# Attention and gated-MLP block on one core: the first loads regrouped, the query weights' means added on VectorE, a longer warm-up on a constant

## The chip, the core and the metric

The kernel runs on one core of a Trainium2 chip. TensorE (PE) multiplies matrices into PSUM; VectorE (DVE), ScalarE (ACT) and GpSimd (POOL) work on SBUF, the first two on PSUM too; SyncE (SP) issues nearly all transfers. The engines run side by side and wait for one another on semaphores. The metric is the device time of one execution in microseconds (us). Three runs of the kernel before took 281.43, 282.21 and 282.88 us, median 282.21.

## The reference

One sequence of 2048 rows of 640, 32 heads of 20. LN is a layer norm without gain or bias; all tensors are bf16.

```
qkv   = LN(x) @ wqkv                         # 640 x 1920
phi(u)= [softmax(u @ w_phi), softmax(-u @ w_phi)]   # 20 + 20 features per head, for q and for k
kv    = sum over rows of phi(k)^T v ,  z = sum over rows of phi(k)
o     = phi(q) kv / (phi(q) z + 1e-6)
h     = x + o @ wo
out   = h + ((LN(h) @ w_gate) * (LN(h) @ w_up)) @ w_down     # 640 x 1536, 1536 x 640
```

## The kernel before, in words

The rows are cut into 16 tiles of 128 (t = 0 to 15) and four blocks of four tiles; the width of 640 into five chunks of 128.

*Weights first.* Since the feature map is linear before its softmax, the kernel multiplies w_phi into the key and query weights once. For the keys (`wk_rounds`, L637) five chunks of the key weights are loaded into `Wnat`, transposed on TensorE against an identity, centred (the mean of each column over the input width is subtracted, which does the layer norm's subtraction of the mean), and multiplied by a block-diagonal `Phi` in the rounds x0 to x4; `evac` (L751) copies each result to `Wp`. For the queries the transposed weights come from five transposing loads (t0 to t4, `wqT`, L1018) into `WT[:, 0]`; `wq_means` (L721, unit wm) makes the column means on TensorE, and ScalarE spreads them over a 128 x 640 tile `nmu`. Each of the rounds y0 to y4 (`wq_round`, L728) then runs twelve matmuls: six on `WT`, six that add the means through `nmu`. The value weights are loaded straight into `Wp`, summed on TensorE (`wv_sums`, unit wv) and centred in place on VectorE (c0 to c4, L776).

*Rows.* x arrives transposed, one transposing load per tile (`load_xT`, L503; lT4 and so on), and again untransposed by blocks (lx0 to lx3). `stats` (units s0, s2, s4, s8, s12) makes the sums and squares of tiles: TensorE, a few small VectorE operations, then seven small GpSimd operations that give each row's scale `rs`. `keys` (k0 to k15) projects a tile (ten matmuls of 320 columns), takes the row's largest absolute value on VectorE (L806, L809), and ScalarE makes two exponentials (L813). The K units sum each head's 40 features on VectorE (L824), invert (L826), and GpSimd multiplies the 128 x 1280 tile (L827). `values` (v0 to v15) projects and ScalarE scales. The units A0 to A14 add up the key-value sums on TensorE, Aout copies them to `KVsb` on VectorE (L893, L896). Queries (q, Q), the quotient (n), the output projection and residual (h), gate and up (f) and down (d, e) follow per block; transposes between them go over SyncE's transposing loads, for tiles 0 and 1 over TensorE.

*What sets the order.* Each engine's order is written out by hand in `ORDER` (L58): a list of unit names per engine, where a name that stands several times stands for that unit's successive operations. `Prog.place` (L200) walks these lists with an assumed duration `t` and latency `lat` for each operation, and settles with them which buffer of a pool an operation gets; the order on an engine is the list's alone. There are four PSUM buffers of two banks. At most eight plain loads and eight transposing loads are in flight, each on a semaphore of its own. Engines issue in order, so an operation that waits holds everything behind it on its engine.

The first units of SyncE's list are all in the unit `in`: five loads of one key-weight chunk each, the value weights in two loads, then the transposed x of tiles 0 to 3. ScalarE issues one load, w_phi. TensorE begins with `warm` (L572): 26 matmuls of 128 columns on the tile `ones`, which GpSimd fills first.

Of the kernel before, what the change touches and what calls it, by code (L numbers as in the profile page):

```python
# [5 lines left out]
FP32 = mybir.dt.float32  # L6
# [5 lines left out]
P = 128  # L12
# [60 lines left out]
    "DVE":  # L73
# [12 lines left out]
    "ACT":  # L86
# [9 lines left out]
    "POOL":  # L96
# [37 lines left out]
class Op:  # L134
    __slots__ = ("eng", "idx", "emit", "deps", "dma", "waits", "vc", "signal", "tick", "sem", "val",
                 "n", "dur", "lat", "bufs", "succ", "start", "end", "open", "bytes", "unit")


class Prog:
# [13 lines left out]
    def op(self, eng, emit, rd=(), wr=(), app=(), dma=None, t=0.2, lat=None, use=(), after=(), size=0.0):  # L153
        o = Op()
        o.eng, o.emit, o.dma = eng, emit, dma
# [44 lines left out]
    def place(self):  # L200
# [20 lines left out]
        while len(order) < len(ops):  # L221
# [29 lines left out]
            if o.dma is not None:  # L251
                land = max(s + 2.3, fabric) + o.bytes
                fabric = land
                o.end = land + o.lat
                flight.setdefault(o.dma[0], []).append(o.end)
            else:
                o.end = s + o.lat
# [119 lines left out]
def _build(ctx, nc, A_x, A_wqkv, A_w_phi, A_wo, B_w_gate, B_w_up, B_w_down, out):  # L377
# [43 lines left out]
    nmean = sb([P, NC], FP32, "nmean")  # L421
    Ssum = sb([P, 2, 2 * H], FP32, "Ssum")
# [9 lines left out]
    nmu, nmuk = [outb[:, k, :].rearrange("p (a n) -> p a n", a=NC) for k in range(2)]  # L432
# [31 lines left out]
    def load(out_, in_, wr, mb, after=(), eng="SP", app=()):  # L464
        return g.op(eng, lambda e: e.dma_start(out_, in_), wr=wr, app=app, after=after, dma=("w", 8), t=0.5, lat=0.4, size=mb / 0.38)  # L465

    def transpose(out_, in_, rd, wr, use=(), t=1.27, size=1.07):

        return g.op("SP", lambda e: e.dma_start_transpose(out_(), in_()), rd=rd, wr=wr, use=use, dma=("tr", 8), t=t, lat=0.5,  # L469
                    size=size)  # L470
# [27 lines left out]
    def load_wnat(w, cs=(0, NC), eng="SP"):  # L498
        c0, c1 = cs
        load(Wnat[:, c0:c1, :], A_wqkv[P * c0:P * c1, D * w:D * (w + 1)].rearrange("(c p) n -> p c n", p=P), R_Wnat[c0:c1],  # L500
             0.16 * (c1 - c0), eng=eng)

    def load_xT(t):  # L503
        transpose(lambda: xT[:, t, :, 0:P], lambda: A_x[0, P * t:P * (t + 1), :], [], [R_xT[t]], t=1.27, size=0.8 if t < 2 else 1.4)

    def load_x(b):
        load(x_all[:, 4 * b:4 * b + 4, :], A_x[0, 4 * P * b:4 * P * (b + 1), :].rearrange("(t p) n -> p t n", p=P), [R_x[b]], 0.64)

    def load_wv(c0, c1):
        load(Wp[:, c0:c1, 2 * D:3 * D], A_wqkv[P * c0:P * c1, 2 * D:3 * D].rearrange("(c p) n -> p c n", p=P), R_Wp[2][c0:c1], 0.16 * (c1 - c0))  # L510

    U("in")
    load(Wrows[:, :, :], A_w_phi.rearrange("h d f -> (h d) f").rearrange("(a p) f -> p a f", p=P), [R_Wrows], 0.03, eng="ACT")
    for c in range(NC):
        load_wnat(1, (c, c + 1))
    load_wv(0, 2)
# [587 lines left out]
```

## Time and profile before

| what | value |
|---|---|
| median of three runs | 282.21 us |
| the profiled execution | 281.24 us, span 279.4 us |
| mean granted TensorE clock | 1.000 |
| TensorE busy | 274.6 us (98%), 2257 matmuls |
| VectorE busy | 165.5 us (59%) |
| ScalarE busy | 133.4 us (48%) |
| GpSimd busy | 106.3 us (38%) |
| transfers | 28.08 MB, mean 100 GB/s |

The span runs from the first to the last instruction of the profiled execution; the 1.8 us between it and the execution's time lie around it. "Busy" is the union of an engine's instructions. Matmuls overlap one another in a pipeline, so a matmul's mean length (299 ns at 320 columns) is longer than the distance from one to the next. In rows of the chain, "SPq" is SyncE's queue of issues and "DMA" the time that a transfer is awaited. Idle time that is shown with "<-" was ended by the instruction behind the arrow.

### The profile page before, as it was taken

What the parts mean: (1) busy time and instruction counts of PE and PEld (TensorE: products, weight loads), DVE (VectorE), ACT (ScalarE), POOL (GpSimd) and SP (SyncE); (2) the same over time, 40 slices, a digit from 0 to 9 for tenths busy, and PEclk for the clock granted to TensorE, in tenths of its full rate; (3) what the DMA queues carried; (4) which work ended last, traced back from release to release, by engine and by line L of the source; (5) the groups of instructions that cost most, each with busy time, mean ns of one, the idle gap of its engine ahead of it and who ended that gap; (6) DMA issues with size and microseconds to landing.
All of it is one profiled execution on the core that took longest, in us unless ns stands there. A gap on an engine that the chain in (4) does not pass through costs nothing.

```text
span 279.4 us, 5540 instructions
## 1 busy us (share of the span) xinstructions
PE 274.6 (98%) x2257; PEld 187.7 (67%) x2257; DVE 165.5 (59%) x313; ACT 133.4 (48%) x227; POOL 106.3 (38%) x156
## 2 busy tenths in 40 slices
PE   8999999999999999999999999999999999999996
PEld 7777778778878888877746655676454444456773
DVE  2999999999899798688528474431141132315011
ACT  2477999998566346363271432401444342410321
POOL 5348899999620322233300680002521034000321
PEclk9999999999999999999999999999999999999999
DMA  7989989404964378946530065561210001000112
GB/s 192 166 170 140 214 125 397 137 2 94 302 78 94 74 180 150 280 99 91 122 73 2 7 136 72 116 98 45 72 49 0 0 0 49 0 0 2 70 48 72
DMA packets 65241, 28.08 MB, mean 100 GB/s; under 512 B 55744, under 2 KB 63936, under 8 KB 65216
## 3 DMA queue, kind: packets, MB, share of 16 engines
q1 hardware_dynamic: 64560, 27.70, 45.8%
q8 instruction: 18, 0.29, 0.5%
q10 hardware_dynamic: 656, 0.03, 0.2%
q14 instruction: 7, 0.06, 0.1%
HBM read 11.82 MB, written 2.62 MB: 52 GB/s over the span
## 4 chain that ended last, share of the span: by engine, by line
PE 94%; SPq 3%; DMA 2%; DVE 1%; issue 0%
PE ps L568 93%; SPq L469 2%; DMA xT<-in_A_x_dram 2%; SPq L465 1%; PE ps L480 0%; DVE outb L1010 0%; DVE KVsb L893 0%; DVE rden L927 0%; DVE KVsb L896 0%
## 5 line engine op out<-in xcount | busy, mean ns | idle before, releaser
L568 PE MATMUL ps<-phik,Wgu 128*128 128x512 bf16 (+1 forms) x600 | 107.6, 336 | 0.0
L568 PEld LDWEIGHTS ps<-phik,Wgu 128*128 128x128 bf16 x600 | 58.2, 98 | 43.6 <-DVE phik L969 1.2
L969 DVE TENSOR_TENSOR phik<-ps,gate 128x512 bf16<-128x512 f32 (+1 forms) x60 | 34.0, 575 | 61.2 <-PE ps L568 60.3
L568 PE MATMUL ps<-Wp,xT 128*128 128x320 bf16 x480 | 68.4, 299 | 0.0
L967 ACT ACTIVATE gate<-ps 128x512 bf16<-128x512 f32 (+1 forms) x60 | 30.1, 512 | 70.4 <-PE ps L568 56.5
L568 PE MATMUL ps<-vaug,phik 128*128 128x320 bf16 (+3 forms) x544 | 60.2, 270 | 0.0
L568 PEld LDWEIGHTS ps<-Wp,xT 128*128 128x128 bf16 x480 | 46.2, 98 | 17.1
L568 PEld LDWEIGHTS ps<-vaug,phik 128*128 128x128 bf16 x544 | 43.4, 97 | 15.9
L985 POOL TENSOR_TENSOR outb<-t,x_all 128x640 bf16<-128x640 f32 x12 | 16.8, 1397 | 88.0 <-ACT t L982 85.7
L827 POOL TENSOR_TENSOR phik<-phik,Rk 128x1280 bf16<-128x1280 bf16 x16 | 37.3, 2357 | 0.7 <-DVE nb L809 0.6
L982 ACT ACTIVATE t<-ps,mh,rs 128x640 f32<-128x640 f32 x12 | 10.6, 882 | 41.4 <-PE ps L568 41.4
L806 DVE TENSOR_REDUCE ps<-ps 128x1 f32<-128x640 f32 x32 | 26.2, 819 | 3.5 <-PE ps L568 3.1
L846 DVE TENSOR_REDUCE Sq<-eq 128x64 f32<-128x1280 bf16 x16 | 23.5, 1474 | 1.6 <-ACT eq L813 1.6
L824 DVE TENSOR_REDUCE Ssum<-phik 128x64 f32<-128x1280 bf16 x16 | 23.4, 1471 | 0.1
L857 POOL TENSOR_TENSOR eq<-eq,rq 128x640 bf16<-128x640 bf16 x16 | 20.3, 1270 | 0.9
L852 POOL TENSOR_TENSOR rq<-Sq,rq 128x32 f32<-128x32 f32 x16 | 4.0, 255 | 39.8 <-DVE rq L851 39.8
L813 ACT ACTIVATE eq<-ps,nb,rs 128x640 bf16<-128x640 f32 x16 | 14.1, 883 | 10.1 <-DVE nb L809 9.3
L813 ACT ACTIVATE phik<-ps,nb,rs 128x640 bf16<-128x640 f32 x16 | 14.0, 884 | 3.1 <-DVE nb L809 3.0
L561 ACT ACTIVATE junk<-x_all 128x640 bf16<-128x640 bf16 x20 | 14.7, 735 | 0.0
L833 ACT ACTIVATE vaug<-ps,rs 128x640 bf16<-128x640 f32 x16 | 12.8, 801 | 3.5 <-PE ps L568 3.5
L813 ACT ACTIVATE eq<-ps,nb,nrs 128x640 bf16<-128x640 f32 x16 | 14.1, 882 | 0.0
L946 DVE SCALAR_TENSOR_TENSOR x_all<-ps,mh,x_all 128x640 bf16<-128x640 f32 x16 | 13.9, 874 | 0.4
(83 smaller groups left out, 226.4 us busy)
## 6 DMA issues: line engine op xcount, KB each, us to landing
x_all<-in_A_x_dram SPq DMA_DIRECT2D x4, 640.0 KB, 9.0
out_dram<-outb SPq DMA_DIRECT2D x15, 160.0 KB, 1.8
Wgu<-in_B_w_up_dram SPq DMA_DIRECT2D x1, 1920.0 KB, 11.3
Wgu<-in_B_w_gate_dram SPq DMA_DIRECT2D x1, 1920.0 KB, 8.2
vaug<-in_B_w_down_dram SPq DMA_DIRECT2D x1, 1920.0 KB, 8.5
phiqT<-in_A_wqkv_dram SPq DMA_DIRECT2D x5, 160.0 KB, 3.8
phiqT<-in_A_wqkv_dram SPq DMA_DIRECT2D x1, 800.0 KB, 6.0
Wo<-in_A_wo_dram SPq DMA_DIRECT2D x1, 800.0 KB, 5.6
```

The lines of the kernel that those rows point to most:

```text
L561: g.op("ACT", lambda e: e.activation(out=junk[:, v.i, :], in_=in_, func=func, accum_out=acc), rd=rd, wr=wr, use=[v], t=0.73, lat=0.97)
L568: ins = e.matmul(o_, lhsT=l_, rhs=r_, start=s_, stop=p_, skip_group_check=True)
L806: g.op("DVE", lambda e: e.tensor_reduce(out=mx(), in_=PS[v.i][:, :, 0:HALF], axis=AX.XY, op=ALU.max, apply_absolute_value=True, negate=Tru ...
L813: g.op("ACT", lambda e, s=s, sc=sc: e.activation(out=signed(dst(), s), in_=PS[v.i][:, :, 0:HALF].rearrange("p b (h f) -> p b h f", f=DH), ...
L824: g.op("DVE", lambda e: e.tensor_reduce(out=Ssum[:, vs.i, :], in_=x, axis=AX.X, op=ALU.add), rd=R_phik[t], wr=vs.R, use=[vs], t=1.39, lat=1.5)
L827: g.op("POOL", lambda e: e.tensor_tensor(out=x, in0=x, in1=Rk[:, vr.i, :].unsqueeze(2).to_broadcast([P, 2 * H, DH]), op=ALU.mult), rd=vr.R ...
L846: g.op("DVE", lambda e: e.tensor_reduce(out=Sq[:, vs.i, :], in_=eq[:, b.i, :].rearrange("p (g f) -> p g f", f=DH), axis=AX.X, op=ALU.add), ...
L857: return e.tensor_tensor(out=x, in0=x, in1=rq[:, vr.i, :].unsqueeze(2).to_broadcast([P, H, DH]), op=ALU.mult)
L946: g.op("DVE", lambda e: e.scalar_tensor_tensor(out=xv, in0=PS[v.i][:, :, 0:HALF], scalar=mh[:, t:t + 1], in1=xv, op0=ALU.subtract, op1=ALU ...
L967: g.op("ACT", lambda e: e.activation(out=gate[:, vg.i, 0:P * n], in_=PS[v.i][:, 0, 0:P * n], func=ACT.Copy), rd=[v.R[0]], wr=vg.R, use=[v, ...
L969: g.op("DVE", lambda e: e.tensor_tensor(out=hhT[:, hb, ft, sl], in0=PS[v.i][:, 1, 0:P * n], in1=gate[:, vg.i, 0:P * n], op=ALU.mult), rd=[ ...
L985: g.op("POOL", lambda e: e.tensor_tensor(out=outb[:, vo.i, :], in0=t32[:, v3.i, :], in1=x_all[:, t, :], op=ALU.add), rd=v3.R + [R_h[t]], w ...
```

## The change

1. The first loads are regrouped. The key weights' five chunks come as three loads: chunks 0 and 1, and chunk 4, on SyncE; chunks 2 and 3 on ScalarE's queue, ahead of w_phi. x of tiles 0 and 1 follows on SyncE, then the value weights in one load, then x of tiles 2 and 3.
2. The query weights' means stay a column of five numbers, `nmeanq`, which ScalarE copies from PSUM. VectorE adds them to the transposed query weights in place, one add of 128 x 640 for each of five chunks (units wq0 to wq4). The tile `nmu` is gone, and a round y runs six matmuls instead of twelve.
3. The warm-up is 34 matmuls, on a constant tile that is there from the start.
4. `Prog.place` assumes other latencies for loads (and given landing times for the first ones), and the five written-out orders are new throughout. On SyncE the query weights (lwq, t0 to t4) now come before x of tiles 8 to 15.

The core of the diff; the orders are cut to their first lines:

```diff
 ORDER = {
     "PE":
-        "warm wk wk wk wk wk wk wk wk wk wk x1 wv x1 x0 x3 wv x0 s0 s0 x2 x4 k0 k0 k0 s2 k0 k0 s2 k1 k3 v1 k2 s4 s4 s4 s4 "
-        "k6 k4 v5 k7 v6 k5 v3 s8 s8 s8 s8 k8 v4 wm v11 k9 v10 k10 s12 v7 s12 s12 s12 y4 y0 y1 y3 k11 y2 k14 v2 q1 q0 v12 "
...
+        "warm wk wk wk wk wk wk wk wk wk wk x1 s0 s0 x1 x0 x3 x0 wv wv x2 s2 x4 s2 k0 k0 k0 k0 k0 k1 k2 v1 s4 s4 s4 s4 k3 "
+        "k5 v6 wm k6 v7 k7 v2 v5 k4 y4 y3 y2 y0 y1 v4 q1 q0 s12 s12 s12 s8 s8 s12 s8 s8 v0 k13 v10 k8 v8 k9 v13 v9 k11 "
...
     "DVE":
-        "wk in in in in in wk wk wk wk x1 x3 c0 s0 s0 s0 c3 c1 c2 s2 s2 s2 k0 k0 c4 k1 k1 k3 K0 k3 k2 k2 s4 s4 s4 s4 s4 "
-        "K1 K0 k4 K1 k4 k6 K3 k6 k7 K3 k7 K2 k5 K2 k5 s8 s8 s8 s8 s8 K4 k8 K4 K6 k8 K5 k9 K6 k9 K8 k10 K5 k10 s12 K7 K8 "
...
+        "wk in in in in in wk wk wk wk s0 s0 s0 x3 x1 c4 c1 s2 c3 s2 s2 k0 c2 k0 c0 k1 k2 k1 K0 s4 k2 s4 s4 K0 s4 k3 s4 "
+        "k3 K1 k5 K2 wq2 k5 wq1 k6 wq0 K2 k6 K1 k7 wq4 k7 K3 wq3 K3 K5 y3 k4 y1 k4 K5 K6 q1 K6 q1 K7 s12 q0 s8 s8 s8 q0 "
...
     "SP":
-        "in in in in in in in in in in in lT4 lT5 lT7 lT6 lx3 lT8 lT11 lT10 lT9 lT15 t0 lT13 lwq t3 lT12 t2 t4 t1 lT14 "
+        "in in in in in in in lT4 lT5 lT6 lT7 lwq t3 t2 t1 t0 t4 lT12 lx3 lT11 lT13 lT9 lT10 lT14 lT8 lT15 lwo lg Q1 Q0 "
...
     U("in")
-    load(Wrows[:, :, :], A_w_phi.rearrange("h d f -> (h d) f").rearrange("(a p) f -> p a f", p=P), [R_Wrows], 0.03, eng="ACT")
-    for c in range(NC):
-        load_wnat(1, (c, c + 1))
-    load_wv(0, 2)
-    load_wv(2, 5)
-    for t in range(4):
-        load_xT(t)
+    load_wnat(1, (2, 4), "ACT", at=4.75)
+    load(Wrows[:, :, :], A_w_phi.rearrange("h d f -> (h d) f").rearrange("(a p) f -> p a f", p=P), [R_Wrows], 0.03, eng="ACT", at=5.5)
+    load_wnat(1, (0, 2), at=4.45)
+    load_wnat(1, (4, 5), at=5.2)
+    load_xT(0, 5.35)
+    load_xT(1, 5.95)
+    load_wv(0, 5, 9.15)
+    for t, at in ((2, 8.95), (3, 9.55)):
+        load_xT(t, at)
...
     def warm(n):
         v = Buf(p_ps, 2)
-        g.op("PE", lambda e: mms(e, [(PS[v.i][:, 0, 0:P], ones[:, :], ones[:, :], True, True) for _ in range(n)]),
-             rd=[R_one], wr=v.R, use=[v], t=0.1 * n, lat=0.1 * n + 0.15)
+        one = nc.const_aps.tensor(1.0, (P, P), BF16)
+        g.op("PE", lambda e: mms(e, [(PS[v.i][:, 0, 0:P], one, one, True, True) for _ in range(n)]),
+             wr=v.R, use=[v], t=0.1 * n, lat=0.1 * n + 0.15)
...
-        g.op("ACT", lambda e: e.activation(out=nmu[:, :, :], in_=PS[v.i][:, 0, 0:NC].unsqueeze(2).to_broadcast([P, NC, P]),
-                                           func=ACT.Copy, scale=-1.0 / SC), rd=[v.R[0]], wr=[R_nmu], use=[v], t=0.61, lat=0.75)
+        g.op("ACT", lambda e: e.activation(out=nmeanq[:, :], in_=PS[v.i][:, 0, 0:NC], func=ACT.Copy, scale=-1.0 / SC),
+             rd=[v.R[0]], wr=[R_nmu], use=[v], t=0.1, lat=0.23)
+        for a in range(NC):
+            U("wq%d" % a)
+            g.op("DVE", lambda e, a=a: e.tensor_scalar(out=WT[:, 0, a, :], in0=WT[:, 0, a, :], scalar1=nmeanq[:, a:a + 1], scalar2=None,
+                                                       op0=ALU.add), t=0.35, lat=0.47, rd=[R_nmu, R_WT[0][a]], wr=[R_WT[0][a]])
...
-        g.op("PE", lambda e: mms(e, part(WT[:, 0, :, P * i:P * (i + 1)], first) + part(nmu, first)), rd=R_WT[0] + R_Phi + [R_nmu],
-             wr=v.R, use=[v], t=0.62, lat=0.77)
+        g.op("PE", lambda e: mms(e, part(WT[:, 0, :, P * i:P * (i + 1)], first)), rd=R_WT[0] + R_Phi,
+             wr=v.R, use=[v], t=0.31, lat=0.46)
...
     U("warm")
-    warm(26)
+    warm(34)
```

More of the change, by code (lines that the diff above doesn't have):

```diff
@@ L135 @@
     __slots__ = ("eng", "idx", "emit", "deps", "dma", "waits", "vc", "signal", "tick", "sem", "val",
-                 "n", "dur", "lat", "bufs", "succ", "start", "end", "open", "bytes", "unit")
+                 "n", "dur", "lat", "bufs", "succ", "start", "end", "open", "bytes", "unit", "at")
 class Prog:
@@ L151, in __init__, with op @@
         self.order = {}
-    def op(self, eng, emit, rd=(), wr=(), app=(), dma=None, t=0.2, lat=None, use=(), after=(), size=0.0):
+    def op(self, eng, emit, rd=(), wr=(), app=(), dma=None, t=0.2, lat=None, use=(), after=(), size=0.0, at=0.0):
         o = Op()
+        o.at = at
         o.eng, o.emit, o.dma = eng, emit, dma
@@ L251, in place @@
             if o.dma is not None:
-                land = max(s + 2.3, fabric) + o.bytes
+                land = o.at or max(s + 2.3, fabric) + o.bytes
                 fabric = land
@@ L421, in _build @@
     nmean = sb([P, NC], FP32, "nmean")
+    nmeanq = sb([P, NC], FP32, "nmeanq")
     Ssum = sb([P, 2, 2 * H], FP32, "Ssum")
@@ L431, in _build @@
     WT = pq[:, NC * D:3 * NC * D].rearrange("p (w a n) -> p w a n", w=2, a=NC)
-    nmu, nmuk = [outb[:, k, :].rearrange("p (a n) -> p a n", a=NC) for k in range(2)]
+    nmuk = outb[:, 1, :].rearrange("p (a n) -> p a n", a=NC)
     vaug = BV[:, :].rearrange("p (t h e) -> p t h e", t=NT, h=H)
@@ L462, in _build, with load, transpose @@
     R_hT, R_oT, R_hhT = [regs(4) for _ in range(2)], [regs(4) for _ in range(2)], [[regs(4) for _ in range(NF)] for _ in range(2)]
[L464 to L470, printed above, removed]
+    def load(out_, in_, wr, mb, eng="SP", at=0.0):
+        return g.op(eng, lambda e: e.dma_start(out_, in_), wr=wr, dma=("w", 8), t=0.5, lat=0.4 if at else 1.9, size=mb / 0.38, at=at)
+    def transpose(out_, in_, rd, wr, use=(), t=1.27, size=1.07, lat=0.5, at=0.0):
+        return g.op("SP", lambda e: e.dma_start_transpose(out_(), in_()), rd=rd, wr=wr, use=use, dma=("tr", 8), t=t, lat=lat,
+                    size=size, at=at)
     def transpose_pe(out_, in_, rd, wr, use, v, bk):
@@ L494, in U, with load_wnat, load_xT, load_wv @@
         g.unit = name
-    def load_wnat(w, cs=(0, NC), eng="SP"):
+    def load_wnat(w, cs=(0, NC), eng="SP", at=0.0):
         c0, c1 = cs
         load(Wnat[:, c0:c1, :], A_wqkv[P * c0:P * c1, D * w:D * (w + 1)].rearrange("(c p) n -> p c n", p=P), R_Wnat[c0:c1],
-             0.16 * (c1 - c0), eng=eng)
-    def load_xT(t):
-        transpose(lambda: xT[:, t, :, 0:P], lambda: A_x[0, P * t:P * (t + 1), :], [], [R_xT[t]], t=1.27, size=0.8 if t < 2 else 1.4)
+             0.3 * (c1 - c0), eng=eng, at=at)
+    def load_xT(t, at=0.0):
+        transpose(lambda: xT[:, t, :, 0:P], lambda: A_x[0, P * t:P * (t + 1), :], [], [R_xT[t]], t=1.5, size=0.75, lat=1.25 if at else 2.75, at=at)
     def load_x(b):
-        load(x_all[:, 4 * b:4 * b + 4, :], A_x[0, 4 * P * b:4 * P * (b + 1), :].rearrange("(t p) n -> p t n", p=P), [R_x[b]], 0.64)
-    def load_wv(c0, c1):
-        load(Wp[:, c0:c1, 2 * D:3 * D], A_wqkv[P * c0:P * c1, 2 * D:3 * D].rearrange("(c p) n -> p c n", p=P), R_Wp[2][c0:c1], 0.16 * (c1 - c0))
+        load(x_all[:, 4 * b:4 * b + 4, :], A_x[0, 4 * P * b:4 * P * (b + 1), :].rearrange("(t p) n -> p t n", p=P), [R_x[b]], 1.2)
+    def load_wv(c0, c1, at):
+        load(Wp[:, c0:c1, 2 * D:3 * D], A_wqkv[P * c0:P * c1, 2 * D:3 * D].rearrange("(c p) n -> p c n", p=P), R_Wp[2][c0:c1], 0.16 * (c1 - c0), at=at)
     U("in")
-    load(Wrows[:, :, :], A_w_phi.rearrange("h d f -> (h d) f").rearrange("(a p) f -> p a f", p=P), [R_Wrows], 0.03, eng="ACT")
-    for c in range(NC):
-        load_wnat(1, (c, c + 1))
-    load_wv(0, 2)
-    load_wv(2, 5)
-    for t in range(4):
-        load_xT(t)
+    load_wnat(1, (2, 4), "ACT", at=4.75)
[7 more added lines that the diff above has]
+        load_xT(t, at)
     def pool_op(f, t, **k):
@@ L1019, in wqT @@
         U("t%d" % a)
-        transpose(lambda: WT[:, 0, a, :], lambda: A_wqkv[:, P * a:P * (a + 1)], [], [R_WT[0][a]], t=1.27, size=1.4)
+        transpose(lambda: WT[:, 0, a, :], lambda: A_wqkv[:, P * a:P * (a + 1)], [], [R_WT[0][a]], t=1.5, size=0.75, lat=2.75)
     U("warm")
-    warm(26)
+    warm(34)
     U("wk")
@@ L1033, in _build @@
     U("lwo")
-    load(Wo[:, :, 0:D], A_wo.rearrange("(c p) n -> p c n", p=P), R_Wo, 0.8)
+    load(Wo[:, :, 0:D], A_wo.rearrange("(c p) n -> p c n", p=P), R_Wo, 1.5)
     for b in range(NB):
```

76 rows, old and new, of the table ORDER are left out of this document.

## The prediction, made before the changed kernel was run

> **What bounds the kernel now.** I read the page's busy shares first (PE 98%), then the chain that ended last, in order of time, because a busy share over pipelined matmuls can't tell streaming from waiting:
>
> ```profile
> 4.12 1.30 SPq L469
> ...
> 6.77 2.20 SPq L469
> ...
> 9.02 4.64 DMA xT<-in_A_x_dram
> 13.65 0.05 issue
> 13.70 62.00 PE ps L568 x670
> ...
> 75.73 0.58 DVE KVsb L893
> ...
> 85.88 190.10 PE ps L568 x1312
> ...
> 276.01 1.02 DVE outb L1010 x2
> ```
>
> Columns: start, length, what. The end is set by three things. A head of 13.7 us: SyncE issues seven weight loads (0.79 to 4.07), then the transposing loads of x, and the fourth of these lands at 13.65. From 13.70 TensorE streams almost without a gap to 276; the one hole is at the key-value sums (0.9 us from 75.73). Then 3.4 us of tail. So a matmul taken out behind 13.7 is worth its full time, if nothing new makes TensorE wait.
>
> Whether something can is told by the busy time by stretch (PE, PEld, DVE, ACT, POOL):
>
> ```profile
> 20.00:30.00 10.00, 10.00 (x83) 7.31 (x80) 9.86 (x24) 8.34 (x12) 7.92 (x10) 1.00 1.16 156
> 30.00:40.00 10.00, 10.00 (x108) 7.70 (x107) 9.27 (x22) 9.36 (x14) 9.15 (x10) 1.00 1.07 174
> 40.00:50.00 10.00, 10.00 (x129) 8.23 (x127) 9.76 (x15) 9.70 (x19) 8.99 (x12) 1.00 0.98 353
> 50.00:60.00 10.00, 10.00 (x76) 7.21 (x74) 9.59 (x16) 9.82 (x16) 9.45 (x5) 1.00 0.17 57
> 60.00:70.00 10.00, 10.00 (x119) 7.83 (x118) 10.00 (x18) 8.96 (x16) 9.92 (x8) 1.00 0.29 66
> ```
>
> VectorE is nearly as full as TensorE here: its idle time in these rows is 0.14 + 0.73 + 0.24 + 0.41 = 1.5 us in 50. A second bound lies about 1 us behind the first, and the change adds work to exactly that engine. GpSimd is 79 to 99% busy, which matters for the second rival.
>
> **The change part by part.**
>
> *Query weights (certain gain).* A round y0 to y4 loses its second half, the six matmuls on `nmu`. In the timeline the halves of four rounds start every 0.315 us (41.84, 42.15, 42.47, ... 44.04), so five rounds lose 5 x 0.315 = 1.57 us. ScalarE's broadcast of the means (L725, 0.72 us) becomes an activation of 5 columns, about 0.2 by its 1-column reads (0.19 to 0.22); nothing waits on ScalarE there, so no gain.
>
> *The five adds (cost on VectorE).* One 640-column bf16 add, in place in SBUF, with a per-partition scalar has no row. Nearest, among the groups by line (busy us, mean ns, idle before); the first row is for the second rival:
>
> ```profile
> L827 POOL TENSOR_TENSOR phik<-phik,Rk 128x1280 bf16<-128x1280 bf16 x16 | 37.3, 2357 | 0.7 <-DVE nb L809 0.6
> ...
> L757 DVE TENSOR_SCALAR Wp<-ps 128x640 bf16<-128x640 f32 x4 | 3.1, 814 | 0.3 <-PE ps L568 0.3
> ...
> L711 DVE TENSOR_SCALAR phiqT<-ps,nmean 128x384 bf16<-128x384 bf16 x3 | 1.1, 412 | 0.1
> ...
> L693 DVE COPY phiqT<-ps 128x640 bf16<-128x640 bf16 x1 | 0.5, 491 | 4.7 <-PE ps L656 4.7
> ```
>
> Between 0.2 (a fixed part alone; L684 with 5 columns takes 0.16) and 0.8 each; I take 0.4, from the bf16 copy of the same width less the 0.08 by which neighbours overlap. Five: 2.0 us, range 1.0 to 4.0. All y rounds read all five results, so y4 waits for the last add. Queued behind each add on VectorE are the max of k5, k6, k7 and the sums of K1 to K3, which ScalarE's exponentials wait for, and those free the PSUM buffers of later TensorE rounds.
>
> Is the last add in time? From the second s2 to y4 TensorE has s2 0.28, k0 k1 k2 v1 and k3 k5 v6 and six more of 1.36 (13 x 1.36 = 17.7), s4 1.14, wm 0.62: 19.7 us. VectorE from its k0 max to wq3: nine maxima and centrings, 0.735 from start to start, four sums by 1.39, three reciprocals by 0.47, s4 0.9, seven small ones by 0.1: 15.2, plus 2.0 for the adds, 17.2; it starts 1.8 after that s2 (k0 must be done). 19.0 against 19.7: it fits by 0.7.
>
> *The loads (head).* SyncE issues two loads before x instead of seven, so x of tile 0 is issued at 0.79 + 2 x 0.46 = 1.7 (was 4.12), tile 1 at 3.0, the value weights at 4.35 as one load of 800 KB, tile 2 at 4.9, tile 3 at 6.2 (7.1 if its predecessor's issue again takes 2.20). Issue to landing was 5.8, 5.0, 5.7 and 4.6 for these four transposes, 5.5 for the 480 KB half of the value weights, 6.0 for the later 800 KB load. Tile 3: 10.8 to 12.8. Value weights: 9.9 to 10.4 by those rows; but they carried the queue in front of them, and less lies ahead now, so 9.0 to 10.4, and I take 9.6. Behind them the new order has wv (10 x 0.136), x2, s2, x4 (0.31 + 0.28 + 0.31): the second s2 starts at 9.6 + 2.27 = 11.9, was 13.70. But k0 (1.36) was done before it and now comes behind it. Head: 13.70 - 11.9 - 1.36 = 0.44 us gained; between +1.0 (s2 at 11.3) and -1.3 (tile 3 lands at 13.65 as now).
>
> *The warm-ups* need no GpSimd memset now, so they start about 0.25 earlier, and eight more at 0.107 (26 took 2.75, from 1.04 to the next operation at 3.79) end at 0.75 + 34 x 0.107 = 4.4. The first weights landed at 3.27 (160 KB); 320 KB in one load, beside as much from ScalarE's queue, land no earlier than the second did, 4.05. So they cost nothing or 0.3 us of a stage that then waits for x and the value weights; without that wait the 0.3 would show.
>
> *ScalarE* issues two loads (0.46 each) ahead of its table load, 0.46 more than now: that ends near 3.0, its first copy ran at 5.37, so nothing. *Moved behind tile 7 on SyncE*: the load and five transposes of the query weights go ahead of tiles 12, 11, 13, 9, 10, 14, 8, 15, and issue costs 1.55 us each there (17.18 to 38.17 for 13 transposes and one load). Tile 8 is issued near 32.5 and lands 4 to 5 later, 36.5 to 37.5; TensorE asks for it at 11.9 + 19.7 + 5 x 0.315 + 3 x 1.36 + 0.4 = 37.7. It fits, by little; if not, up to 1 us. Wq's own load: 14.2 + 6.0 = 20.2, wm runs at 22.8. *The rest of the order*: same operations, no new dependency, so I cost it at nothing.
>
> *Where the stall goes next.* At the key-value sums VectorE was ready 1.2 us before TensorE (it waits 1.2 at 74.58). Now TensorE comes 1.57 + 0.44 = 2.0 earlier. VectorE gets 2.0 (adds) and 0.74 (one more centring behind the k0 max), starts 1.0 earlier (13.7, was 14.69), and can win back 1.0 to 1.8 of the 1.85 us that it idles between 14 and 70. So it is ready between 0.1 earlier and 0.7 later than now, and TensorE, 2.0 earlier, waits for it: 0.7 to 1.5 us of the gain go there. All four copies of the sums now stand together, which returns 0.7 of the 2.04 us between the first copy and the next matmul. Net at that point: 1.2 to 2.0 gained, I take 1.6. Behind it TensorE streams 200 us with other engines free, so this survives to the end. **Sum:** the profiled execution took 281.24 (span 279.4, 1.8 around it); 281.24 - 1.6 = 279.6. The median of the runs is 0.97 above that execution, so I expect **280.6** against 282.21.
>
> **The rivals.**
>
> *A. The head doesn't come forward.* If the transfers, not their issue, limit the head, tile 3 still lands near 13.65, and the k0 moved behind it costs what the y rounds save: 1.57 - 1.36 = 0.2 gained, and up to 0.5 lost if VectorE is late too: 282.0, or 281.7 to 282.7. For it: the busy share of the DMA engines is 7 to 9 tenths over the first 49 us. Against: tile 2 and 3 landed 1.1 to 2.0 apart while a transpose needs 0.6 to 0.8 when queued (tiles 0 and 1, 9.94 and 10.51): issue held them up. The Trainium skill (DMA: Bandwidth & Descriptors, "Issuing engines are not separate DMA queues") says that a second issuing engine saves only the time of the issue. By that rule the ScalarE queue alone is worth one issue, 0.4 us, and the sum would be this rival's, 282; no run here shows it.
>
> *B. The adds wait for GpSimd (slower).* The adds may be held while a GpSimd multiply of the keys (2.357 us) runs. In the new orders K0's multiply starts behind s4's chain and overlaps wq2 (about 1.0 held); K2's starts 1.3 before wq4 (1.1 held); K1's starts as wq4 ends, 1.5 before wq3 (0.9 held). wq1 and wq0 fall into a GpSimd gap, since K2's reciprocal comes behind them. That is 3.0 us on VectorE: wq3 ends 2.3 after TensorE wants y4, and the key-value sums come 3.0 later: 280.6 + 3.0 = 283.6, and 285 if the hold hits all five. It decides from about 1.6 us of holding. The trace can't exclude it: no VectorE row of before reads and writes bf16 in SBUF with one tensor source, and the rows that exist don't stretch (the reciprocals L826, 540 to 544 ns, all under GpSimd work). The Trainium skill (SBUF — State Buffer, "Who interferes with whom") states it as a rule: VectorE in a two-port mode and GpSimd lock one port pair against each other for a whole instruction, and a bf16 scalar add in SBUF is such a mode; no run here shows it.
>
> **How the numbers follow.** Forecast 0.47 (279.4 to 281.6), A 0.22, B 0.31. Half a per cent, 1.4 us, is about what a measurement can tell. Faster: 0.7 of the forecast's and a little of A, 0.38. Slower: three quarters of B and a little of A, 0.29. Same 0.33. The range takes the forecast's lower end with a start of 11.3 (278.8) up to B with some more holding (284.2).
>
> **What would show it.** Right: y rounds of six matmuls; the second s2 near 11.9 and k0 straight behind; no TensorE wait before y4; the wait at the key-value sums no longer than now. B: wq rows over 1 us that end with a GpSimd multiply, and TensorE idle before y4. A: second s2 at 13 or later. Wrong for another reason: a TensorE wait at s8 for x of tile 8, or at s4.

## The result, and the profile after

The changed kernel takes 283.47 us (median of 22 runs, 282.91 to 288.44); the kernel before, run beside it, 282.34 (22 runs, 281.24 to 284.31). The ratio is 1.0055, with a 95% interval of 1.0037 to 1.0073: slower by half a per cent, where 280.6 was forecast. It is what rival B said (283.6).

The profiled execution of the changed kernel is one of its longest, 286.63 us, because one load came late in it (at the end of this document). A second profile of the same kernel, 283.00 us (span 281.3), has the usual length; the readings below go by that one, and the first is shown where both say the same.

The chain of waits of the 286.63 us execution, in order of time (start, length, what):

```profile
4.97 6.90 DMA Wp<-in_A_wqkv_dram
...
11.92 12.28 PE ps L572 x102
24.22 0.83 DVE ps L815
...
28.76 1.67 DVE phiqT L734
...
33.43 1.33 DVE phiqT L734
...
36.35 0.94 DVE phiqT L734
...
39.09 0.73 DVE Wp L766
39.83 0.05 issue
39.88 40.96 PE ps L572 x446
...
90.79 190.68 PE ps L572 x1322
```

Before, the chain lay on TensorE from 13.70 to 75.7 in one piece. Now it leaves TensorE at 24.2 and stays on VectorE, mostly, until 39.8: VectorE sets the pace of that stage, and L734, the adds, are among its longest pieces. The groups by line of the same execution (busy us, mean ns, idle before) give their size:

```profile
L836 POOL TENSOR_TENSOR phik<-phik,Rk 128x1280 bf16<-128x1280 bf16 x16 | 37.5, 2360 | 5.7 <-DVE nb L818 3.1 <-DVE Rk L835 2.4
...
L734 DVE TENSOR_SCALAR phiqT<-phiqT,nmeanq 128x640 bf16<-128x640 bf16 x5 | 5.0, 995 | 0.0
```

5.0 us for five adds, where 2.0 was forecast. A mean of 995 ns hides that they are of two kinds. The timeline of VectorE in the 283.00 us execution (start, length) shows every one:

```profile
24.99 1.67 DVE L734 TENSOR_SCALAR phiqT<-phiqT,nmeanq 128x640 bf16<-128x640 bf16 x1
...
26.65 0.37 DVE L734 TENSOR_SCALAR phiqT<-phiqT,nmeanq 128x640 bf16<-128x640 bf16 x1
...
27.67 0.37 DVE L734 TENSOR_SCALAR phiqT<-phiqT,nmeanq 128x640 bf16<-128x640 bf16 x1
...
29.58 1.54 DVE L734 TENSOR_SCALAR phiqT<-phiqT,nmeanq 128x640 bf16<-128x640 bf16 x1
...
32.51 1.01 DVE L734 TENSOR_SCALAR phiqT<-phiqT,nmeanq 128x640 bf16<-128x640 bf16 x1
```

and that of GpSimd at the same time its key multiplies:

```profile
24.11 2.36 POOL L836 TENSOR_TENSOR phik<-phik,Rk 128x1280 bf16<-128x1280 bf16 x1
28.58 4.75 POOL L836 TENSOR_TENSOR phik<-phik,Rk 128x1280 bf16<-128x1280 bf16 x2 [2.11 <-DVE nb L818]
```

Three adds begin inside a multiply and end 0.18 to 0.19 us after it: 26.66 against 26.47, 31.12 against 30.94 (the first of the pair), 33.52 against 33.33. The two that fall into GpSimd's gap (26.47 to 28.58) take 0.37. Together 4.96 instead of 5 x 0.37 = 1.85: 3.1 us of holding. TensorE's timeline of the same execution shows what ended its waits, with the idle time in brackets:

```profile
28.38 4.25 PE L572 MATMUL ps<-Wp,xT 128*128 128x320 bf16 x30 [0.43 <-ACT vaug L842]
33.58 1.12 PE L572 MATMUL ps<-Phi,phiqT 128*128 128x140 bf16 x18 [0.94 <-DVE phiqT L734]
34.86 0.49 PE L572 MATMUL ps<-Phi,phiqT 128*128 128x140 bf16 x6 [0.17 <-ACT Wp L763]
36.10 0.49 PE L572 MATMUL ps<-Phi,phiqT 128*128 128x140 bf16 x6 [0.76 <-DVE Wp L766]
```

Matmuls overlap, so the delay from one start to the next is longer than the idle time: TensorE loses 0.59 before v2, 1.11 before y4 (for wq3), 0.33 before y0 and 0.92 before y1 (for VectorE's copy of y3, itself late), 3.0 in all, where the kernel before waited for nothing. Not all of the 3.0 is the hold's: e2, below, keeps 0.5 of it. The busy time by stretch of the same execution (PE, PEld, DVE, ACT, POOL, clock, share of the DMA engines, GB/s):

```profile
20.00:30.00 10.00, 9.57 (x91) 6.70 (x89) 9.93 (x20) 7.51 (x12) 5.92 (x8) 1.00 1.09 190
30.00:40.00 10.00, 8.13 (x77) 5.82 (x75) 10.00 (x13) 8.60 (x15) 7.58 (x4) 1.00 0.81 206
```

TensorE was 10.00 in both stretches before. VectorE's 10.00 in the second is no sign of work done: a held instruction counts as busy.

The head came as forecast. The value weights landed at 9.63, the fourth x at 10.90, the second s2 started at 11.96.

### The profile page after: what moved, and what is told of

The parts are those of the page before. It is cut to its first block, busy times and chain, and to the rows that moved or that the text cites. A ratio compares the mean times of both kernels' runs of the same rounds, so it can differ in the third digit from the quotient of the medians.

```text
span 284.9 us, 5493 instructions
## 1 busy us (share of the span) xinstructions
PE 275.8 (97%) x2235; PEld 186.7 (66%) x2235; DVE 168.8 (59%) x318; ACT 133.7 (47%) x227; POOL 106.4 (37%) x156
## 4 chain that ended last, share of the span: by engine, by line
PE 86%; DVE 7%; DMA 2%; SPq 1%; issue 1%; ACT 1%; POOL 1%
PE ps L572 86%; DMA Wp<-in_A_wqkv_dram 2%; DVE phiqT L734 2%; DVE ps L815 2%; DVE Ssum L833 1%; SPq L471 1%; ACT eq L822 1%; DVE Sq L855 0%; DVE Rk L835 0%; DVE ob L938 0%; POOL eq L866 0%; DVE outb L1019 0%; SPq L467 0%; DVE Wp L766 0%; DVE rden L936 0%
## 5 line engine op out<-in xcount | busy, mean ns | idle before, releaser
L961 POOL TENSOR_SCALAR vpe<-shc 128x1 f32<-128x1 f32 x16 | 3.0, 190 | 46.0 <-ACT junk L565 44.9
L822 ACT ACTIVATE phik<-ps,nb,nrs 128x640 bf16<-128x640 f32 x16 | 14.3, 895 | 0.0
L936 DVE RECIPROCAL rden<-ps 128x32 f32<-128x32 f32 (+1 forms) x18 | 5.7, 324 | 14.5 <-PE ps L572 14.5
```

What stands on the lines that cost most here:

```text
L822: g.op("ACT", lambda e, s=s, sc=sc: e.activation(out=signed(dst(), s), in_=PS[v.i][:, :, 0:HALF].rearrange("p b (h f) -> p b h f", f=DH), ...
```

## The experiments

Each kernel is timed in five rounds against the kernel before on the same chip, whose median was 282.04, 282.30 and 282.10 us in the three groups (e1 to e4, e5 to e8, e9 to e12). The second group ran on another chip than the first and the third, so between groups the ratios compare better than the medians. "Loses" is TensorE's time from one matmul's start to the next beyond its own streaming time. In the diffs, an order is cut to the names around the edit.

| label | what | median us (runs) | ratio, 95% interval |
|---|---|---|---|
| e1_after_again | the changed kernel | 283.01 (12) | 1.0030 [1.0004, 1.0055] |
| e2_no_multiply | four GpSimd multiplies left out | 280.73 (12) | 0.9957 [0.9934, 0.9981] |
| e3_adds_together | adds in one group, early | 282.74 (12) | 1.0017 [0.9994, 1.0041] |
| e4_head_of_before | old head | 285.34 (7) | 1.0101 [1.0063, 1.0140] |
| e5_head_alone | new head, the rest as before | 281.95 (12) | 0.9995 [0.9976, 1.0014] |
| e6_adds_in_a_gap | adds where no multiply runs | 282.58 (12) | 1.0009 [0.9988, 1.0029] |
| e7_adds_one_hold | adds in one group, later | 280.96 (12) | 0.9960 [0.9942, 0.9979] |
| e8_adds_other_form | adds of two tensors | 286.36 (6) | 1.0152 [1.0115, 1.0189] |
| e9_no_adds | adds left out | 280.63 (12) | 0.9952 [0.9929, 0.9975] |
| e10_adds_with_sum | adds that also sum | 283.20 (12) | 1.0043 [1.0010, 1.0075] |
| e11_gap_third_buffer | e6 with one more buffer | 281.23 (12) | 0.9964 [0.9943, 0.9985] |
| e12_one_hold_old_head | e7 with the old head | 282.21 (12) | 1.0018 [0.9992, 1.0043] |

### Is it the multiply that holds the adds?

**e1** is the changed kernel with no edit, to stand beside the others.

> The changed kernel once more, unaltered, for a profile beside the others and for how much its head varies. In its first profile (286.6 us) TensorE lost 2.4 us waiting for the value weights, which landed at 11.88, about 1.4 us more at a half-rate clock behind that, and 3.0 us around the query weights (0.6 before v2, 1.1 before y4, 0.3 before y0, 0.9 before y1). Theory lock: GpSimd's running multiply holds three of the five adds; that loss stands in every execution, whatever the head does: wq rows of about 0.37 us twice and 1.0 to 1.7 us three times again, 283.0 to 283.6 us. Theory head: the late value weights are the loss; then a fast execution has them near 10 and no loss around y, and the holds vary.

Measured 283.01, with the rows shown above.

**e2** takes away what the adds would wait for:

```diff
+        if t < 4:
+            return
         g.op("POOL", lambda e: e.tensor_tensor(out=x, in0=x, in1=Rk[:, vr.i, :].unsqueeze(2).to_broadcast([P, 2 * H, DH]), op=ALU.mult),
```

> The changed kernel without GpSimd's multiplies of the keys of tiles 0 to 3 (their features stay unscaled, so the output is not the reference's); VectorE's work is unchanged. Theory lock: all five adds take about 0.37 us, wq3 ends 3 us earlier, TensorE doesn't wait before y4 and y1, and the time is 2 to 3 us under the changed kernel, about 280.5 to 281. Rival, the adds are long by themselves (mean 0.995 us, read from SBUF at whatever rate): the rows stay at 0.4 to 1.7, the time within 0.7 us of the changed kernel's. Rival head: rows shorten but the time stays, since another wait takes over.

Measured 280.73, 2.3 below e1. All five adds take 0.37, y4 starts at 31.97 (33.58 in e1) without a wait, and of the 3.0 us that TensorE lost between v2 and y1, 0.5 is left (0.23 and 0.27, at the y rounds). So the adds are held by GpSimd's multiplies, or by something that goes when they go. e2 alone can't tell the hold from a GpSimd that is free for other work; e7 and e10, which keep the multiplies, can.

**e9** leaves the adds out and keeps the multiplies:

```diff
-        for a in range(NC):
-            U("wq%d" % a)
-            g.op("DVE", lambda e, a=a: e.tensor_scalar(out=WT[:, 0, a, :], in0=WT[:, 0, a, :], scalar1=nmeanq[:, a:a + 1], scalar2=None,
...
```

> The changed kernel without the five adds (the query weights stay uncentred; six-matmul y rounds, GpSimd's multiplies as they are). With this and the kernel with one short hold, the price of the adds splits into their own work (five times 0.29 from start to start and the wait at the end, 1.5 on VectorE) and the hold. If only the hold costs time: equal to that kernel, 280.7 to 281.0. If the adds' own 1.5 us on VectorE costs too, as a full VectorE would have it: 279.5 to 280.0.

Measured 280.63: level with e2. Without adds, or with adds that nothing holds, the time is the same. The adds' own 1.5 us on VectorE are hidden; the 3.1 of holding are not.

### Does the place of the adds decide?

**e3** puts the five adds together where the first stood:

```diff
-  K1 k5 K2 wq2 k5 wq1 k6 wq0 K2 k6 K1 k7 wq4 k7 K3 wq3 K3
+  K1 k5 K2 wq2 wq1 wq0 wq4 wq3 k5 k6 K2 k6 K1 k7 k7 K3 K3
```

> The changed kernel with the five adds one behind the other at the place of the first; all else in its order. Theory lock: only the first can meet a running multiply (up to 2 us), the other four take 0.37 or less, so VectorE loses 0.5 to 2 us there in place of 3.1; 281.4 to 282.4 us. If GpSimd's next multiply gets in between, one more is held. Rival, long by themselves: five times about 1 us, no change in time, 283.0 to 283.6.

Measured 282.74. One add is held (25.07 to 26.73, to the end of tile 0's multiply), the four behind it take 0.37: the group of five lasts 2.85 us in all. The holding fell from 3.1 to 1.3 and hardly anything was won, because the group stands ahead of k5's centring. ScalarE's exponentials of k5 start later, v7's scaling behind them too, and TensorE waits 1.78 before v2 for the PSUM buffer.

**e7** moves the group behind the centring of k5 and the max of k6:

```diff
-  K1 k5 K2 wq2 k5 wq1 k6 wq0 K2 k6 K1 k7 wq4 k7 K3 wq3 K3
+  K1 k5 K2 k5 k6 wq2 wq1 wq0 wq4 wq3 K2 k6 K1 k7 k7 K3 K3
```

> The whole change, with the five adds behind the centring of k5 and the max of k6, in one group, ahead of tile 2's reciprocal; GpSimd's order stays. The first add starts near 25.7 to 26.2 while tile 0's multiply runs to 26.5: held to about 26.7, the other four 0.37. By the hold theory with k5's exponentials no longer late: one hold of 0.5 to 1.0 is left of 3.1, TensorE loses at most 0.3 before y4 and nothing before v2: 281.2. If a hold costs the same wherever it stands: 282.7 as when the adds stood together ahead of k5.

Measured 280.96, faster than both kernels: ratio to the kernel before 0.9960 [0.9942, 0.9979]. It does all the work of the changed kernel in another order. Its timelines of GpSimd and VectorE:

```profile
24.01 2.35 POOL L836 TENSOR_TENSOR phik<-phik,Rk 128x1280 bf16<-128x1280 bf16 x1
28.27 6.99 POOL L836 TENSOR_TENSOR phik<-phik,Rk 128x1280 bf16<-128x1280 bf16 x3 [1.91 <-DVE nb L818]
```

```profile
25.91 1.82 DVE L734 TENSOR_SCALAR phiqT<-phiqT,nmeanq 128x640 bf16<-128x640 bf16 x5
```

The five begin 0.45 before tile 0's multiply ends (26.36) and end before the next one starts. Five in a row without a hold would take 4 x 0.29 + 0.37 = 1.53, so 0.3 is left of the hold. TensorE loses nothing before v2 and 0.75 at the y rounds. In e1 and e7 the instructions are the same on every engine; only the order on VectorE differs, and with it how many adds meet a multiply. The difference is 2.05 us by the medians and 2.0 by the ratios. It is the price of the hold together with what k5 and k6 gain by standing ahead of the adds (e3 shows that this counts); e2 (2.3) and e9 (2.4), which leave VectorE's other work in its order, put the price at about the same.

**e6** changes GpSimd's order as well, so that no multiply runs beside an add:

```diff
 POOL
-  K0 K2 K1 K3
+  K2 K0 K1 K3
 DVE
-  K1 k5 K2 wq2 k5 wq1 k6 wq0 K2 k6 K1 k7 wq4 k7 K3 wq3 K3
+  K1 k5 K2 wq2 k5 wq1 k6 wq0 wq4 wq3 K2 k6 k7 k7 K3 K1 K3
```

> The whole change, with another order: GpSimd multiplies the keys of tile 2 ahead of tile 0, and the five adds stand ahead of the reciprocal that this multiply needs, so that no GpSimd multiply of the keys runs while the adds do. The same operations as the changed kernel, nothing left out. If the hold by the multiply is the whole cost: all five adds at 0.37, TensorE doesn't wait before y4, 280.7 as with the multiply left out, up to 281.2 if GpSimd, 2.4 later, delays something. If it was the missing multiply's work as such that made that run fast (GpSimd free, not VectorE unheld): 282.5 to 283.

Measured 282.58, a miss. All five adds took 0.37 to 0.38, as wanted, and the gain was lost at another place. VectorE's timeline, with the idle time before the row in brackets:

```profile
33.00 0.55 DVE L835 RECIPROCAL Rk<-Ssum 128x64 f32<-128x64 f32 x1 [1.79 <-POOL phik L836]
```

The reciprocals have two buffers. With tile 0's multiply put off, a reciprocal on VectorE waits for GpSimd to free one; behind it stand the sum of K3 and the copy of y3, which now ends at 35.62 (33.59 in e7). So y3 keeps its PSUM buffer for 2 us more. v4 starts at 35.66, when this copy and ScalarE's of y0 (to 35.60) are both done, and TensorE loses 0.98 ahead of it.

**e11** is e6 with a third buffer (in the output tile, free at that time):

```diff
+    Rk3 = [Rk[:, 0, :], Rk[:, 1, :], outb[:, 0, 0:4 * H].bitcast(FP32)]
...
-        g.op("DVE", lambda e: e.reciprocal(out=Rk[:, vr.i, :], in_=Ssum[:, vs.i, :]), ...
+        g.op("DVE", lambda e: e.reciprocal(out=Rk3[vr.i], in_=Ssum[:, vs.i, :]), ...
```

> The kernel whose adds stand in GpSimd's gap (tile 2's multiply ahead of tile 0's), with a third buffer for the reciprocals, so that VectorE's reciprocals don't wait for GpSimd. If the 1.79 us that VectorE waited at the reciprocal ahead of y3 was what took the gain of the unheld adds: 280.8. If it was something else (the later multiplies, the head): 282 to 282.6 again.

Measured 281.23: the 1.35 us came back (1.3 by the ratios), so the buffer was the reason. e6 and e11 together say that a hold can be moved into a wait on another resource as easily as removed.

### Which adds are held?

**e8** writes the add as one of two tensors, the second the means repeated:

```diff
-  e.tensor_scalar(out=WT[:, 0, a, :], in0=WT[:, 0, a, :], scalar1=nmeanq[:, a:a + 1], scalar2=None, op0=ALU.add)
+  e.tensor_tensor(out=WT[:, 0, a, :], in0=WT[:, 0, a, :], in1=nmeanq[:, a:a + 1].to_broadcast([P, D]), op=ALU.add)
```

> The changed kernel with the five adds as an add of two tensors, the second the column of means repeated 640 times, at the same places in the order. One such add without GpSimd beside it is estimated at 0.75 (0.82 for the max of 640 columns). If only the form with one tensor and a scalar column is held: five times 0.75, none longer when the multiply runs, wq3 ends 1.2 earlier than at 33.5, TensorE loses 0 to 0.3 before y4: 281.5 to 282. If any VectorE operation that reads and writes SBUF in bf16 is held: three rows stretched to 1.2 to 1.7 and the rest 0.75, 283.5.

Measured 286.36, a miss beyond both expectations. In VectorE's and GpSimd's timelines:

```profile
25.09 2.16 DVE L734 TENSOR_TENSOR phiqT<-phiqT,nmeanq 128x640 bf16<-128x640 bf16 x1
...
27.24 0.81 DVE L734 TENSOR_TENSOR phiqT<-phiqT,nmeanq 128x640 bf16<-128x640 bf16 x1
```

```profile
24.21 2.35 POOL L836 TENSOR_TENSOR phik<-phik,Rk 128x1280 bf16<-128x1280 bf16 x1
30.06 5.25 POOL L836 TENSOR_TENSOR phik<-phik,Rk 128x1280 bf16<-128x1280 bf16 x2 [3.49 <-DVE nb L818]
```

This form takes 0.81 by itself and is held too (2.16, 2.05 and 1.51 beside the multiplies); it ends about 0.7 after the multiply. The hold works the other way as well: the two multiplies in a row take 5.25 here and 4.75 in e1, where an add that waited for the first runs on into the second, and 4.67 in e11, where none does. wq3 comes 2.5 later than in e1, and TensorE waits 2.9 before y4. Two things lie beyond the expectation: the held rows are longer than the 1.2 to 1.7 that it allowed, and the clock fell. After that wait the granted clock stood at 0.5 for 6.8 us, as the busy time by stretch shows in part:

```profile
38.00:40.00 2.00, 1.53 (x11) 1.08 (x11) 1.87 (x3) 1.22 (x3) 0.89 (x1) 0.50 1.03 411
40.00:42.00 2.00, 2.00 (x9) 1.16 (x8) 2.00 (x4) 1.68 (x3) 1.17 (x1) 0.50 1.04 401
42.00:44.00 2.00, 2.00 (x10) 1.13 (x8) 0.09 (x1) 1.38 (x3) 1.18 (x1) 0.53 0.52 201
```

**e10** uses the form of the scalar add that also writes each row's sum:

```diff
-  e.tensor_scalar(out=WT[:, 0, a, :], in0=WT[:, 0, a, :], scalar1=nmeanq[:, a:a + 1], scalar2=None, op0=ALU.add)
+  e.tensor_scalar(out=WT[:, 0, a, :], in0=WT[:, 0, a, :], scalar1=nmeanq[:, a:a + 1], scalar2=0.0, op0=ALU.add, op1=ALU.add,
+                  accum_out=wsum[:, a:a + 1])
```

> The changed kernel with the adds in the form that also writes each row's sum (to a column that nothing reads), at the same places in the order. If the hold belongs to the fast form of the add (0.37 for 640 columns, which this form is not expected to reach): five rows of 0.7 to 0.85, none longer beside a multiply, 3.5 to 4.2 in place of 4.98 on VectorE, 281.8 to 282.3. If any add in SBUF is held, as the add of two tensors was: rows of 2.2, 2.1 and 1.5 where the multiply runs, 286.

Measured 283.2, over two groups: six runs from 282.24 to 282.70, six from 283.71 to 287.54. The profiled one is the last, with late value weights as in the first profile of the changed kernel, so its times are shifted; but its rows tell the form apart:

```profile
28.51 0.87 DVE L734 TENSOR_SCALAR_CACHE_REDUCE phiqT<-phiqT,nmeanq 128x640 bf16<-128x640 bf16 x1
```

```profile
27.64 2.35 POOL L837 TENSOR_TENSOR phik<-phik,Rk 128x1280 bf16<-128x1280 bf16 x1
```

The add begins and ends inside the multiply and takes 0.87, like the other four (0.86 to 0.87, and 0.08 for reading the sum), of which one lies outside any multiply. This form is not held. At 0.87 each, five cost 0.6 less than in e1, and the six shorter runs, with a median of 282.37, are 0.6 below e1's 283.01, near the expected 281.8 to 282.3; that the late load made the other six longer is shown by one profile only. TensorE's wait before v2 is gone in this execution, those before y4 (1.11) and y1 (0.93) are not: 4.3 us of adds that nothing holds cost nearly what the 5.0 of e1 cost. This points to the time on VectorE, held or not, as what counts.

So the fast scalar add and the add with two inputs in SBUF are held, and the slower scalar add with a sum, the sums over features (1.48 beside a multiply and without one) and the reciprocals (0.54) are not. The Trainium skill (SBUF — State Buffer, "Who interferes with whom") draws the line in this way: two-port modes and two SBUF inputs share a port pair with GpSimd, reductions and the scalar form that writes its accumulator don't. These runs agree, with the numbers just given.

### What is the head worth?

**e4** gives the changed kernel the head of the kernel before (loads and orders up to the second s2; the 34 warm-ups stay):

```diff
-    load_wnat(1, (2, 4), "ACT", at=4.75)
...
-    load_wv(0, 5, 9.15)
+    for c in range(NC):
+        load_wnat(1, (c, c + 1))
+    load_wv(0, 2, 0.0)
+    load_wv(2, 5, 0.0)
+    for t in range(4):
+        load_xT(t)
```

> The head of the kernel before (its first loads in its order, and all engines' orders up to the second s2 and k0), and behind it the rest of the changed kernel: query weights by five adds, rounds y of six matmuls, its orders; the warm-up stays at 34. Theory lock: the loss around y stays as it is in the changed kernel, and what this version differs by is the head alone. With the head of before (k0 nearly done at 13.7) against the changed one (second s2 at 11.9 in a good execution, 15.7 in the profiled one): from 0.4 us slower to 3 us faster than the changed kernel; I expect 0.5 to 1 us faster, 282.5. Theory head: it takes the whole loss back and keeps the 1.6 us of the rounds y: 280.7.

Measured 285.34, a miss by 2.8. Up to x of tile 1 the loads went out at the same times as in the kernel before, and landed later: x of tile 1 at 12.46 (10.51 before), so TensorE lost 0.95 before wv and 1.16 before s0, and the second s2 started at 15.29 instead of 13.70. The first add was held for longer too (wq2 2.3 us).

**e5** is the converse, the new head with 34 warm-ups on the kernel before:

```diff
-    for c in range(NC):
-        load_wnat(1, (c, c + 1))
...
+    load_wnat(1, (2, 4), "ACT", at=4.75)
...
-    warm(26)
+    warm(34)
```

> The changed head (loads in three and one pieces, x of tiles 0 and 1 ahead of the value weights, 34 warm-ups on the constant, the new order up to the second s2) with everything behind it as before: twelve-matmul y rounds on the spread means, no adds. If the changed head is worth what the prediction took from it, the second s2 starts near 12.0 (13.70 before), k0 (1.36) comes behind it, and the time is 0.4 under the kernel before: 281.6. If it is worth nothing because the stages behind it are not ready earlier, 282.0 to 282.3. If it costs something by itself, above 282.5, and then part of the loss of the changed kernel is the head's and not the adds'.

Measured 281.95, ratio 0.9995 [0.9976, 1.0014]: at most a little gained. The second s2 starts at 12.17, k0 behind it. The chain of waits of e5 shows where a gain would have gone:

```profile
12.17 8.40 PE ps L571 x75
...
21.36 2.34 ACT phik L817 x3
...
24.51 0.78 ACT phik L817
25.30 0.05 issue
25.34 4.66 PE ps L571 x33
```

TensorE, earlier now, loses 0.88 before k7, waiting for ScalarE's exponentials.

**e12** is e7 with the whole old head, 26 warm-ups on the filled tile included:

```diff
-    load_wnat(1, (2, 4), "ACT", at=4.75)
...
+    for c in range(NC):
+        load_wnat(1, (c, c + 1))
...
-    warm(34)
+    warm(26)
```

> The kernel with one short hold, with the whole head of the kernel before (seven loads, 26 warm-ups on the filled tile, its order up to the second s2). If the old head is as good as it was in the kernel before (fourth x at 13.65, second s2 at 13.70, 1.36 of k0 done ahead of it): 281.4, 0.4 behind the new head. If its loads land late as in the earlier run of this head (value weights 8.39, x of tile 1 12.46): 283.3, and the 34 warm-ups on the constant were not the reason.

Measured 282.21, between the two expectations; the fastest runs are at 281.5, its profiled one, among its two longest, at 284.10, with the first part of the value weights at 9.09 (7.23 before). So the new head is worth 1.2 us by the medians, 1.6 by the ratios, with e7's order behind it (280.96 against 282.21) and 0.35 or nothing with the old order (e5). Why the old head's loads land later with the new order behind them, up to 2 us in e4, stays open: the issue times up to x of tile 1 are the same, and the warm-ups are not the reason alone.

## Why the prediction was wrong, by its own steps

- **The five adds, "I take 0.4".** This step failed. The width was right: 0.37 by itself. But the bound of 0.8 for one add was no bound, since it came from rows that nothing holds. Measured were 1.67, 1.54 and 1.01 for three of five, each to the end of a GpSimd multiply. The sentence "19.0 against 19.7: it fits by 0.7" fell with it: 3.1 more on VectorE, 1.11 us of wait before y4.
- **Rival B** had the mechanism, the three adds that meet a multiply (wq2, wq4, wq3) and the two that don't. It put the holds at 1.0, 1.1 and 0.9; they were 1.30, 1.17 and 0.64, 3.1 against 3.0. Its time, 283.6, stands against 283.0 to 283.5, but it charged all 3.0 of holding to the time, where 2.0 to 2.4 were charged (e7, e2, e9). "It decides from about 1.6 us of holding" was too simple: e3 had 1.3 of holding and was 0.7 us slower than the kernel before on that chip by the medians (interval across no change), because that hold stood ahead of k5's centring. It was given 0.31, too little. The two orders were on paper and showed the overlap; what was missing was a row that showed the lock, and "the rows that exist don't stretch" was read as evidence against it, though the rows named (reciprocals with one source) are of a kind that is never held.
- **The y rounds, −1.57.** Right in TensorE's own work: the head alone (e5) and the changed kernel differ by 1.57 us of streaming. But five rounds of 0.31 now follow each other faster than their copies out of PSUM (0.71 on ScalarE, 0.81 on VectorE, in turn), and even in e7 TensorE loses 0.75 there. No step of the prediction had that wait; it takes back half of the gain.
- **The head, +0.44.** Right in place: value weights at 9.63 (forecast 9.6), x of tile 3 at 10.90 (10.8 to 12.8), second s2 at 11.96 (11.9). Rival A's condition, a second s2 at 13 or later, did not come. By itself the head gained next to nothing in time (e5), since ScalarE was late at k7.
- **The warm-ups, 0 or 0.3.** The first matmuls on the key weights start at 4.72 (3.79 before), 0.93 later: the loads of two chunks land at 4.67 and 5.01, later than one of one chunk, and not near the 4.05 that the step took as their earliest. Mis-sized, but hidden, as the step said: TensorE then waits for the value weights.
- **"Net at the key-value sums: 1.6".** Wrong place. TensorE lost 0.71 there before and 0.58 after; VectorE was not the later there. The gain was lost earlier (the y rounds) and a little later: the units n3 wait 0.3 to 0.7 for ScalarE's exponential of q4, which before cost nothing.
- **Tile 8, ScalarE's two loads, the rest of the order at nothing.** TensorE didn't wait for x of tile 8, nor for ScalarE's first copies. The rest of the order can't be told apart from the losses at the y rounds and n3.

Without the hold the time is near the forecast: 280.63 (adds left out), 280.73 (multiplies left out) and 280.96 (moved) against 280.6. The 2.0 to 2.4 us between these and 283.0 is the step that failed.

That the rest of the sum comes out is in part luck. From profile to profile these three are only 0.4 to 0.6 us shorter than the kernel before (spans 279.0, 278.9 and 278.8 against 279.4), not 1.6; the waits at the y rounds and at n3, 1.1 to 1.2 us together, which the sum didn't have, account for most of the difference. **The 0.97** made up for it: the sum added it because the median of the kernel before lay that far above its profiled execution, which is the shortest of its 22 runs; in these three the median lies 0.08 below, 0.05 above and 0.45 above the profiled one. A size that was too large and an offset that did not carry over nearly cancel. Why the executions of the kernel before scatter more stays open, since there is one profile of it.

## What to carry to other kernels

Before a VectorE operation is added beside a busy GpSimd, look in the timeline at what GpSimd runs at that moment: a fast SBUF-to-SBUF form was held here to the end of a GpSimd multiply, however short it is by itself, so its price is what is left of GpSimd's instruction and not its own duration. Put such operations together, in a gap of GpSimd's, and behind what another engine waits for; the same five adds cost 2 us or almost nothing by their place alone. A bound from the nearest rows is only a bound if these rows meet the same neighbour.

## What the runs showed of the hardware that was not expected

- A wait of TensorE can cost twice. At waits of 1.8 (e12), 2.2 (e10), 2.4 (first profile of the changed kernel) and 2.9 us (e8) the granted clock fell to 0.5, for 3.4 us in the first three and 6.8 in e8, and matmuls of 320 columns started 267 ns apart instead of 136. The length of one wait doesn't decide it: the 1.8 us before v2 in e3 left the clock at 1.00, and so did the waits from y4 to y1 in e1 (1.11, 0.33, 0.92), but the same three in e10 were followed by another 3.4 us at 0.5. What decides was not tried. In the 286.63 us execution, by stretch:

```profile
8.00:12.00 4.00, 1.75 (x33) 1.57 (x31) 2.56 (x9) 1.12 (x2) 0.51 (x5) 0.96 1.25 188
12.00:14.00 2.00, 2.00 (x8) 1.08 (x9) 0.00 (x0) 0.00 (x0) 0.00 (x0) 0.50 1.63 64
```

- One load can be late by the last few of its packets. In that execution the 800 KB of value weights landed at 11.88 (9.63 in the usual one). Nearly all its packets had started by 9.6; the last 28, of 1280 bytes, started one after another, 52 ns apart, from 10.04 to 11.43, and the transposing load behind it, x of tile 2, landed at 14.06 instead of 10.29. Five packets in a quarter of a microsecond, where about 70 went before, look like one DMA engine of the 16, but the trace doesn't name a packet's engine. The waits of TensorE's weight loads in that execution (us in total, times, longest) name it:

```profile
PEld ps L572 <- DMA Wp<-in_A_wqkv_dram: 2.4, 1, 2.4
```

  e10's profile shows the same tail, with the value weights at 11.57. In e12 the first of the old head's two loads is late too (9.09), but there the packets thin out gradually. What makes the last packets late in some executions was not tried and stays open.
